# Retention in 64-column tiles of the array: padded queries, key halves, one retention step per filler

## The chip, the cores and the metric

The kernel runs on one core of one Trainium2 chip. The metric is device time in microseconds of one launch, median of several runs. A core has five engines with a queue of instructions each: TensorE (PE, matrix products; PEld is its loading of weights), VectorE (DVE), ScalarE (ACT), GpSimd (POOL) and SyncE (SP), which here issues nearly all DMA transfers. TensorE writes to PSUM, which is eight banks of 128 partitions; VectorE and ScalarE take results out of it.

## The reference

Eight batches of 576 tokens. First retention with 8 heads of 64: causal, decaying scores without a softmax. Its output goes through an attention with 4 experts of which 2 are chosen per token, and then through a token and channel mixer (last lines left out here).

```python
gamma = 1.0 - 2.0 ** (-5.0 - np.arange(H))
rel = pos[:, None] - pos[None, :]
Dmat = np.where(rel >= 0, gamma[:, None, None] ** rel[None, :, :], 0.0)
ret = scale * np.matmul(q, k.transpose(0, 1, 3, 2)) * Dmat[None]
x = np.matmul(ret, v)                 # 8 batches x 8 heads x 576 x 64
# then, per expert e: q, k, v = x @ wq[e], x @ wk[e], x @ wv[e]
#   a = softmax(causal(q @ k.T / 8)); out += gate_e * (a @ v @ wo[e])
# then theta = x @ w_theta; y = w_tok_r @ (x cos theta) + w_tok_i @ (x sin theta)
#   u = x + y; result = u + relu(u @ w_ch)
```

The inputs of the three parts are independent of the kernel's tiling; only retention is touched by the change.

## The kernel before

The program has two halves. The first does retention, projections and attention for batch after batch; the second (from about 560 us) is the mixer. In the first half the attention of batch b runs as 10 units (2 pairs of experts x 5 row chunks), and beside it, as fillers, the second pair's projections of batch b and then retention, values and first projections of batch b+1. `fill` takes fillers off a list by cost numbers until the share of the batch is done. What is issued is then set in its final order, engine by engine, by the framework's scheduler, so instructions of neighbouring pieces are interleaved.

Retention works in 5 chunks of 128 rows (the last has 64), `ROWS`. Heads go in pairs: head pair hp (0 to 3) has two heads s, whose 64 dimensions lie in partitions 0 to 63 and 64 to 127.

- `loads(b, c)` (L95): one DMA brings queries and keys `qk`, transposed, one DMA brings rows of keys and values `kv`; GpSimd scales values into `vp` (L102). Three buffers each; the loads of a chunk are issued at the end of the output of the chunk three before.
- `ret_scores` (L106): for each head a product of 64 contraction rows, keys (128 columns) by queries (128), L113. A matmul on half the array's rows leaves the other half to the other head. The two heads of a pair go to two PSUM tiles `w`. VectorE multiplies each tile with the triangle `tri` into `sm` (L117). The quarter of keys above 64 by queries under 64 is computed and then zeroed.
- `ret_out` (L121): keys by values are added to the running state in PSUM `pS` (L130, 64-column tiles, one head in columns 0 to 63 of the array and one in 64 to 127); ScalarE copies the state into a block-diagonal `S` (L135, two copies, the rest of `S` is zero from the start). The output tile `w` collects state times queries (L139, the whole array, 128 columns of weights) and `vp` times `sm` (L143, 64-column tiles). VectorE multiplies with the decay into `xt` (L150), ScalarE and GpSimd split it (L152, L153).

PSUM holds four tiles `a` for attention, three `w` (`WB`) for retention and projections, and `pS`. Around these, TensorE runs the attention: scores L258 (`KK`, whole array) and L261 (`KL`, half the rows), transposes of the probabilities `P` L310, attention output L329 (64-column tiles), and projections L83 to L85. VectorE takes the scores' maxima (L264), scales `P` (L283), and copies transposed tiles (L315, L317).

All products of retention are float32, which TensorE runs as two passes; a trace shows each pass as a matmul with a weight load.

Of the kernel before, what the change touches and what calls it, by code (L numbers as in the profile page):

```python
# [20 lines left out]
E, DM = 4, 512  # L21
# [6 lines left out]
NCONST = 256 + NCH * H + 1088 + E * E + 4 * (128 + NCH)  # L28
# [25 lines left out]
def tile_kernel(ctx: ExitStack, tc: tile.TileContext, qk, kv, w1, wo, wot, wd, cst, out):  # L54
# [17 lines left out]
    tri = att.tile([128, 128], F32, name="tri")  # L72
# [7 lines left out]
    SB = [ret.tile([128, 4, 128], F32, name=f"S{i}") for i in range(2)]  # L80
# [14 lines left out]
    def loads(b, c):  # L95
        R = ROWS[c]
        t = ret.tile([128, 2, 4, R], F32, name="qk", bufs=LDB, padded_shape=[128, 2, 4, 128])
        nc.sync.dma_start(t, qk[b, :, c * 1024:c * 1024 + 8 * R].rearrange("p (a h r) -> p a h r", a=2, h=4))
        u = ret.tile([128, 2, DM], F32, name="kv", bufs=LDB)
        nc.sync.dma_start(u[:R], kv[b, c * C:c * C + R, :].rearrange("r (a d) -> r a d", a=2))  # L100
        vp = ret.tile([128, H, D], F32, name="vp", bufs=VPB)
        MARK["pool"] = nc.gpsimd.tensor_mul(vp[:R], u[:R, 1, :].rearrange("p (h d) -> p h d", h=H),  # L102
                             gam[:R, c, :, None].to_broadcast([R, H, D]))
        QKT[b, c], KVT[b, c], VP[b, c] = t, u, vp

    def ret_scores(b, c):  # L106
        R = ROWS[c]
        t, u = QKT[b, c], KVT[b, c]
        ps = [ps1.tile([128, 4, R], F32, name="w", bufs=WB, padded_shape=[128, 4, 128]) for _ in range(2)]
# [4 lines left out]
        sm = []  # L114
        for s in range(2):
            m = ret.tile([128, 4, R], F32, name="sm", bufs=3, padded_shape=[128, 4, 128])
            nc.vector.tensor_mul(m[:R], ps[s][:R], tri[:R, None, :R].to_broadcast([R, 4, R]))  # L117
            sm.append(m)
        SM[b, c] = sm

    def ret_out(b, c):  # L121
        R = ROWS[c]
        t, u, vp, sm = QKT.pop((b, c)), KVT.pop((b, c)), VP.pop((b, c)), SM.pop((b, c))
# [34 lines left out]
    def ret_fill(b):  # L158
        L = []
        for c in range(NCH + 1):  # L160
            if c < NCH:
                L.append((1.74, lambda c=c: ret_scores(b, c)))
# [602 lines left out]
```

## Time and profile before

| | us |
|---|---|
| runs | 998.91, 1000.17, 998.31; median 998.91 |
| span of the profiled execution | 994.0 |
| PE busy | 964.6 (97%) |
| PEld busy | 857.6 (86%) |
| DVE busy | 677.7 (68%) |
| ACT busy | 499.9 (50%) |
| POOL busy | 221.9 (22%) |

The profiled execution lists its span, from the first to the last instruction; the runs' times hold what lies around it as well. A busy share is an average over stages. In the chain of waits, which is followed back from the last instruction, each piece is what the span was waiting for at that moment; a piece named "issue" is time in which the engine waited for nothing that the profile shows.

### The profile page before, as it was taken

Reading aid. Unit: us, or ns where it says so; the run is one execution under the profiler, and the core shown is the slowest. Engines: PE = TensorE matmul, PEld = TensorE weight load, DVE = VectorE, ACT = ScalarE, POOL = GpSimd, SP = SyncE. Lnnn points to the kernel's source line nnn. Section 1 sums busy time; section 2 is a strip of 40 time slices with the busy share of each in tenths; the row PEclk is TensorE's granted clock in tenths of the full one; section 3 lists DMA queues with packets and bytes.
Section 4 is the critical chain, followed back from the end, with each engine's and each line's share of the span. In section 5 each row is a group of like instructions: output and inputs, shape, how many; then the busy total and the mean of one; then the engine's idle time right before and its main releaser. Section 6 shows DMA issues by size and latency. Waiting matters only on the chain.

```text
span 994.0 us, 20992 instructions
## 1 busy us (share of the span) xinstructions
PE 964.6 (97%) x7898; PEld 857.6 (86%) x7898; DVE 677.7 (68%) x2035; ACT 499.9 (50%) x1310; POOL 221.9 (22%) x270
## 2 busy tenths in 40 slices
PE   7999999999999999999999999999999999999998
PEld 6978878788787887887867799999999999999998
DVE  6387897878777878778566793485655746486533
ACT  3366676666664766667566661344333432344320
POOL 4244262352532623423000002020100102020110
PEclk9999999999998999999999999999999999999999
DMA  9454573554544635443641301010000101000001
GB/s 308 153 155 150 144 211 82 161 174 134 173 124 118 217 100 155 161 133 112 251 150 36 122 1 48 2 72 25 25 24 24 49 1 48 2 36 13 25 25 48
DMA packets 58293, 99.27 MB, mean 100 GB/s; under 512 B 13904, under 2 KB 35792, under 8 KB 58192
## 3 DMA queue, kind: packets, MB, share of 16 engines
q1 hardware_dynamic: 58048, 97.65, 31.2%
q8 instruction: 62, 1.02, 0.4%
q0 software_dynamic: 144, 0.28, 0.1%
q14 instruction: 39, 0.32, 0.1%
HBM read 65.09 MB, written 23.66 MB: 89 GB/s over the span
## 4 chain that ended last, share of the span: by engine, by line
PE 88%; DVE 5%; DMA 2%; ACT 2%; issue 2%; SPq 0%; ACTq 0%; DVEq 0%
PE acc L641 23%; PE w L83 12%; PE w L84 11%; PE w L85 11%; PE a L329 5%; PE a L310 5%; PE w L113 4%; PE a L258 3%; PE w L143 3%; PE a L261 3%; PE w L139 2%; PE acc L631 2%; PE pS L130 1%; DMA qk<-qk 1%; DVE P L283 1%
## 5 line engine op out<-in xcount | busy, mean ns | idle before, releaser
L641 PE MATMUL acc<-TK,zh 128*128 128x256 f32 (+1 forms) x1024 | 183.8, 302 | 0.0
L641 PEld LDWEIGHTS acc<-TK,zh 128*128 128x128 f32 x1024 | 152.4, 190 | 0.7 <-DVE ul L89 0.2
L667 POOL TENSOR_TENSOR o<-o,ul 128x576 f32<-128x576 f32 x28 | 41.8, 1499 | 436.1 <-DVE o L662 436.1
L269 ACT ACTIVATE P<-P,st 128x128 f32<-128x128 f32 (+4 forms) x160 | 95.6, 599 | 72.2 <-DVE st L264 71.8
L641 PE MATMUL acc<-TK,zl 128*128 128x256 f32 (+1 forms) x512 | 110.0, 297 | 0.0
L264 DVE CUSTOM_DVE_ANT_0 P<-a,cm 128x128 f32<-128x128 f32 (+4 forms) x160 | 72.3, 478 | 49.7 <-PE a L261 49.1
L641 PEld LDWEIGHTS acc<-TK,zl 128*128 128x128 f32 x512 | 86.2, 189 | 0.1
L585 ACT ACTIVATE cs<-cs 128x512 f32<-128x512 f32 x72 | 45.2, 630 | 80.4 <-DVE cs L583 76.7
L88 ACT ACTIVATE zh<-cs 128x512 fp32r<-128x512 f32 x64 | 40.2, 630 | 81.3 <-PE acc L641 66.9
L89 DVE TENSOR_TENSOR zl<-cs,zh 128x512 fp32r<-128x512 f32 x64 | 45.0, 707 | 50.4 <-ACT zh L88 49.5
L83 PE MATMUL w<-xh,WH 128*128 128x288 f32 x256 | 79.0, 308 | 0.0
L84 PE MATMUL w<-xl,WH 128*128 128x288 f32 x256 | 76.4, 299 | 0.0
L84 PE MATMUL w<-ul,CH 128*128 128x256 f32 (+1 forms) x256 | 75.9, 296 | 0.0
L83 PE MATMUL w<-uh,CH 128*128 128x256 f32 (+1 forms) x256 | 75.9, 296 | 0.0
L85 PE MATMUL w<-uh,CH 128*128 128x256 f32 (+1 forms) x256 | 75.9, 296 | 0.0
L85 PE MATMUL w<-xh,WL 128*128 128x288 f32 x256 | 75.7, 296 | 0.0
L587 DVE SCALAR_TENSOR_TENSOR cs<-cs,x 128x512 f32<-128x512 f32 x72 | 55.4, 776 | 24.6 <-ACT cs L585 24.5
L310 PE MATMUL a<-ident,P 128*128 128x128 f32 (+2 forms) x480 | 63.4, 264 | 7.8 <-DVE P L283 6.2
L113 PE MATMUL w<-qk 64*128 64x128 f32 (+1 forms) x640 | 59.1, 277 | 10.8 <-issue 5.6
L113 PEld LDWEIGHTS w<-qk 64*128 64x128 f32 (+1 forms) x640 | 50.8, 180 | 18.2 <-issue 10.5
L89 DVE TENSOR_TENSOR ul<-acc,uh 128x256 fp32r<-128x256 f32 x64 | 25.7, 451 | 59.3 <-ACT uh L88 59.1
L117 DVE TENSOR_TENSOR sm<-w,tri 128x512 f32<-128x512 f32 (+1 forms) x80 | 49.6, 629 | 21.6 <-PE w L113 11.4
(139 smaller groups left out, 2466.6 us busy)
## 6 DMA issues: line engine op xcount, KB each, us to landing
qk<-qk SPq DMA_DIRECT2D x32, 512.0 KB, 4.6
kv<-kv SPq DMA_DIRECT2D x32, 512.0 KB, 3.9
KK<-KN SPq DMA_DIRECT2D x64, 144.0 KB, 2.5
raw<-wd SPq DMA_DIRECT2D x43, 192.0 KB, 2.7
out<-o SPq DMA_DIRECT2D x28, 288.0 KB, 2.1
td<-hl SPq DMA_DIRECT2D x27, 192.0 KB, 2.3
TK<-td SPq DMA_DIRECT2D x9, 576.0 KB, 6.9
od<-ob SPq DMA_DIRECT2D x16, 288.0 KB, 2.6
```

The source lines that it names most:

```text
L83: nc.tensor.matmul(ps, ah, bh, start=first, stop=False)
L84: nc.tensor.matmul(ps, ah, bl, start=False, stop=False)
L85: nc.tensor.matmul(ps, al, bh, start=False, stop=last)
L89: nc.vector.tensor_sub(l, src, h)
L113: nc.tensor.matmul(ps[s][:R, hp, :], t[sl, 1, hp, :], t[sl, 0, hp, :], start=True, stop=True)
L117: nc.vector.tensor_mul(m[:R], ps[s][:R], tri[:R, None, :R].to_broadcast([R, 4, R]))
L264: MARK["dve"] = nc.vector.tensor_tensor_reduce(Ps[s][:R, j0:j1], ps[s][:R], cm[:R, o + j0:o + j1], 1.0, st[:R, 0, s:s + 1] if i else 3.0e3 ...
L269: MARK["act"] = nc.scalar.activation(Ps[s][:R, :n], Ps[s][:R, :n], AF.Exp, bias=st[:R, last, s:s + 1], scale=-1.0, accum_out=st[:R, 2, s:s ...
L310: nc.tensor.transpose(tp[:w, j, :], Ps[s][:R, j * C:j * C + w], ident[:R, :R])
L329: nc.tensor.matmul(po[s * 64:s * 64 + 64, c0:], V[:ROWS[j], j, 2 * p + s, :], v, start=j == 0, stop=j == last, skip_group_check=True)
L587: nc.vector.scalar_tensor_tensor(z, cs, -1.0, x2[:, None, ds].to_broadcast([128, 2, 256]), op0=OP.mult, op1=OP.mult)
L641: nc.tensor.matmul(acc[d][j], A[:, dc], TK[:, kt, W, t0:t1], start=q == 0 and n == 0, stop=q == 8 and n == 2)
```

## The change

Every product of retention now has 128 contraction rows and 64 columns of weights.

- Queries go to `QZ`, three fixed buffers with two planes: plane s holds the queries of head s in its 64 partitions and zeros in the other 64. The zeros are written once, at the start, by GpSimd. One load of `qk` becomes three: two of queries (64 partitions each) and one of keys, `kt`.
- Scores: weights are 64 keys of both heads of a pair (128 rows), the queries of both planes stream side by side: 2 x 128 columns for the first 64 keys, 2 x 64 for the second 64, which skip the queries under 64. The halves alternate between the left and right 64 columns of the array. Odd head pairs have their key halves swapped in the PSUM partitions, and so `kv` and the decay table are swapped for them on the host. The rows of the last chunk's `kv` are padded to 128.
- Masks: four VectorE instructions instead of two per chunk (two for the last chunk), into fixed tiles `SMT` whose unseen quarter is zeroed once.
- State: `S` is 64 columns wide and no longer block-diagonal: ScalarE copies it in one instruction. State times queries is one product per head with that head's plane, 64 columns of weights.
- `ret_fill` gives one filler per chunk, scores of chunk c and output of chunk c-1, where these were two; the cost numbers are lower.

```diff
     def loads(b, c):
...
+        qz = QZ[(b * NCH + c) % LDB]
+        for s in range(2):
+            sl = slice(s * 64, s * 64 + 64)
+            nc.sync.dma_start(qz[sl, s, :, :R], qk[b, sl, o:o + 4 * R].rearrange("p (h r) -> p h r", h=4))
...
     def ret_scores(b, c):
...
-        for hp in range(4):
-            for s in range(2):
-                sl = slice(s * 64, s * 64 + 64)
-                nc.tensor.matmul(ps[s][:R, hp, :], t[sl, 1, hp, :], t[sl, 0, hp, :], start=True, stop=True)
-        for s in range(2):
-            nc.vector.tensor_mul(m[:R], ps[s][:R], tri[:R, None, :R].to_broadcast([R, 4, R]))
+        for i in range(2):
+            for e, j in ((0, 0), (1, 0), (1, 1), (0, 1)):
+                if j * 64 < R:
+                    g = slice((e ^ j) * 64, (e ^ j) * 64 + 64)
+                    hp = 2 * i + e
+                    nc.tensor.matmul(ps[e][g, i, :, j * 64:R], t[:, hp, j * 64:j * 64 + 64],
+                                     qz[:, :, hp, j * 64:R], start=True, stop=True, skip_group_check=True)
+        for e in range(2):
+            g = slice(e * 64, e * 64 + 64)
+            nc.vector.tensor_mul(sm[e][g, :, :, :64], ps[e][g, :, :, :64],
+                                 tri[g, 2, None, None, :].to_broadcast([64, 2, 2, 64]))
+            if R > 64:
+                nc.vector.tensor_mul(sm[e][:, :, :, 64:], ps[e][:, :, :, 64:],
+                                     tri[:, e, None, None, :].to_broadcast([128, 2, 2, 64]))
...
     def ret_out(b, c):
...
-            Sn = SB[(c + 1) % 2]
-            for s in range(2):
-                sl = slice(s * 64, s * 64 + 64)
-                nc.scalar.activation(Sn[sl, :, sl], pS[sl], AF.Copy)
+            nc.scalar.activation(SB[(c + 1) % 2], pS, AF.Copy)
...
-            nc.tensor.matmul(px[:, hp, :], Sb[:, hp, :], t[:, 0, hp, :], start=hp == 0, stop=False,
-                             skip_group_check=True)
+            for s in range(2):
+                nc.tensor.matmul(px[s * 64:s * 64 + 64, hp, :], Sb[:, hp, :], qz[:, s, hp, :R],
+                                 start=hp == 0, stop=False, skip_group_check=True)
...
     def ret_fill(b):
...
-                L.append((1.74, lambda c=c: ret_scores(b, c)))
...
-                L.append((2.9, lambda c=c: ret_out(b, c - 1)))
+        return [((1.4 if c < NCH else 0) + (2.5 if c else 0), lambda c=c: step(c)) for c in range(NCH + 1)]
```

In the order of instructions a name is the tile written, an arrow, the tiles read; the shape is that of the result, and a number behind x counts equal neighbours. The lines of the new kernel are other ones: its scores are L125, keys by values L146, state L153, outputs L157, attention L272, L275, L324, L343, masks L130 and L133, and L164 the decay.

TensorE, third batch's retention, from the first scores to the third. Before:

```order
L85 MATMUL w<-xh,WL 128x288
L113 MATMUL w<-qk 128x128 x16
L329 MATMUL a<-PT,V 64x128 x2
L258 MATMUL a<-KK,U 128x384 x2
L261 MATMUL a<-KL,U 128x384 x2
L310 MATMUL a<-ident,P 128x128 x4
L130 MATMUL pS<-vp,kv 64x64 x8
L143 MATMUL w<-sm,vp 64x128 x8
L113 MATMUL w<-qk 128x128 x4
```

After, from the end of the first scores:

```order
L125 MATMUL w<-qz_109,kt 64x256 x2
L125 MATMUL w<-qz_109,kt 64x2x64 x2
L343 MATMUL a<-PT,V 64x128 x2
L272 MATMUL a<-KK,U 128x384 x2
L275 MATMUL a<-KL,U 128x384 x2
L324 MATMUL a<-ident,P 128x128 x4
L125 MATMUL w<-qz_110,kt 64x256 x2
L125 MATMUL w<-qz_110,kt 64x2x64 x2
L125 MATMUL w<-qz_110,kt 64x256 x2
L125 MATMUL w<-qz_110,kt 64x2x64 x2
L146 MATMUL pS<-vp,kv 64x64 x8
```

The scores of chunks 0 and 1, sixteen neighbours before, now have the attention's pieces between them.

TensorE, the same batch, scores of chunk 3 and output of chunk 2. Before:

```order
L113 MATMUL w<-qk 128x128 x2
L310 MATMUL a<-ident,P 128x128 x8
L113 MATMUL w<-qk 128x128 x6
L130 MATMUL pS<-vp,kv 64x64 x8
L139 MATMUL w<-qk,S_107 128x128 x4
L143 MATMUL w<-sm,vp 64x128 x8
L258 MATMUL a<-KK,U 128x128 x2
```

After:

```order
L125 MATMUL w<-qz_109,kt 64x256
L324 MATMUL a<-ident,P 128x128 x8
L125 MATMUL w<-qz_109,kt 64x256
L125 MATMUL w<-qz_109,kt 64x2x64 x2
L125 MATMUL w<-qz_109,kt 64x256 x2
L125 MATMUL w<-qz_109,kt 64x2x64 x2
L146 MATMUL pS<-vp,kv 64x64 x8
L153 MATMUL w<-qz_111,S_107 64x128 x8
L157 MATMUL w<-sm_114,vp 64x128 x2
```

From the scores to the outputs all rows now are 64 high; before, the height and the operands' rows change at each line. The transposes still cut into the scores.

VectorE at the start of the same batch's retention. Before:

```order
L283 TENSOR_SCALAR P<-P,st 128x256
L194 SCALAR_TENSOR_TENSOR U<-w,U 64x288 x2
L117 TENSOR_TENSOR sm<-w,tri 128x512 x3
L264 ISA P,st<-a,cm 128x384
L264 ISA st 128x1
L264 ISA P,st<-a,cm 128x384
L264 ISA st 128x1
L315 COPY PT<-a 128x2x128
```

After:

```order
L297 TENSOR_SCALAR P<-P,st 128x256
L208 SCALAR_TENSOR_TENSOR U<-w,U 64x288 x2
L130 TENSOR_TENSOR sm_114<-w,tri 64x4x64
L133 TENSOR_TENSOR sm_114<-w,tri 128x4x64
L130 TENSOR_TENSOR sm_115<-w,tri 64x4x64
L133 TENSOR_TENSOR sm_115<-w,tri 128x4x64
L278 ISA P,st<-a,cm 128x384
L278 ISA st 128x1
L278 ISA P,st<-a,cm 128x384
L278 ISA st 128x1
L329 COPY PT<-a 128x2x128
L130 TENSOR_TENSOR sm_112<-w,tri 64x4x64
```

Three masks of 512 columns stood ahead of the attention's maxima; now the four of one chunk do, and the next chunk's four come behind.

## Rows read from the trace of the kernel before

**Rows 1.** The page's busy time of TensorE and its weight loads, others behind.

```profile
PE 964.6 (97%) x7898; PEld 857.6 (86%) x7898; DVE 677.7 (68%) x2035; ACT 499.9 (50%) x1310; POOL 221.9 (22%) x270
```

**Rows 2.** Busy time by stage: the start, three of seven retention stretches, sum of seven.

```profile
core 0: us, PE busy (x) PEld busy (x) DVE busy (x) ACT busy (x) POOL busy (x), PEclk, DMA share, GB/s
0.00:30.00 30.00, 23.90 (x313) 21.69 (x314) 17.61 (x25) 10.41 (x18) 13.38 (x19) 1.00 0.91 304
...
175.00:207.20 32.20, 30.83 (x349) 25.39 (x349) 26.69 (x93) 21.41 (x60) 15.62 (x20) 1.00 0.61 190
238.00:270.00 32.00, 28.50 (x304) 23.40 (x306) 25.96 (x81) 18.54 (x53) 12.44 (x15) 0.95 0.55 162
306.00:338.00 32.00, 30.64 (x314) 24.70 (x314) 26.57 (x86) 19.35 (x55) 14.72 (x18) 0.89 0.53 165
...
sum 225.20, PE 213.24 PEld 173.61 DVE 189.19 ACT 143.76 POOL 97.80; mean PE 30.46 PEld 24.80 DVE 27.03 ACT 20.54 POOL 13.97
```

**Rows 3.** Chain of waits, 176 to 206 us: start, us, what, passes.

```profile
176.64 1.14 PE w L113 x16
177.78 1.18 issue
178.96 1.83 PE w L113 x16
...
182.66 0.61 PE pS L130 x16
183.28 0.88 PE w L143 x16
...
188.34 0.62 DVE P L283
...
189.87 0.45 PE w L139 x4
...
196.86 1.09 PE w L139 x8
197.95 1.02 PE w L143 x16
...
200.22 0.61 PE w L113 x16
```

**Rows 4.** Waits, 49 to 500 us: who for whom, us in total, times, longest.

```profile
PEld w L113 <- issue: 10.5, 22, 1.4
PE a L310 <- DVE P L283: 6.2, 9, 2.1
PE w L113 <- issue: 5.6, 5, 1.2
```

**Rows 5.** Chain of waits, single pieces of three other stretches.

```profile
16.40 6.72 DMA qk<-qk
...
128.53 1.08 PE a L329 x12
...
257.35 2.51 DVE P L283
```

**Rows 6.** Groups by shape: count, busy us, mean ns of one, idle before.

```profile
L117 DVE TENSOR_TENSOR sm<-w,tri 128x512 f32<-128x512 f32 x64 | 43.1, 685 | 18.3 <-PE w L113 11.4 <-PE w L143 6.2 <-PE a L261 0.4
L117 DVE TENSOR_TENSOR sm<-w,tri 64x256 f32<-64x256 f32 x16 | 6.5, 407 | 3.3 <-PE w L143 3.3
L264 DVE CUSTOM_DVE_ANT_0 P<-a,cm 128x256 f32<-128x256 f32 x32 | 12.5, 422 | 13.9 <-PE a L261 13.9
L135 ACT ACTIVATE S<-pS 64x256 f32<-64x256 f32 x64 | 24.1, 377 | 2.8 <-PE pS L130 2.3
L347 POOL MEMSET S<- 128x512 f32 x2 | 1.0, 524 | 0.3 <-POOLq L757 0.3
```

**Rows 7.** Issues of line L98: ns least, median, most; first and last start.

```profile
L98 SPq DMA_DIRECT2D qk<-qk x40: 327/358/562, 1.2 to 450.5; - x40
```

**Rows 8.** Weight loads of line L143, the same columns.

```profile
L143 PEld LDWEIGHTS w<-sm,vp x640: 128/137/231, 10.0 to 467.7; 128*64 128x64 f32 x128, 64*64 64x64 f32 x32
```

More of the change, by code (lines that the diff above doesn't have):

```diff
@@ L71, in tile_kernel @@
     ident = consts.tile([128, 128], F32, name="ident")
-    tri = att.tile([128, 128], F32, name="tri")
+    tri = att.tile([128, 3, 64], F32, name="tri")
     gam = att.tile([128, NCH, H], F32, name="gam")
@@ L79, in tile_kernel @@
     gt = ret.tile([128, 4, S], F32, name="gt")
-    SB = [ret.tile([128, 4, 128], F32, name=f"S{i}") for i in range(2)]
+    SB = [ret.tile([128, 4, D], F32, name=f"S{i}") for i in range(2)]
+    QZ = [ret.tile([128, 2, 4, 128], F32, name=f"qz{i}") for i in range(LDB)]
+    SMT = [[ret.tile([128, 2, 2, 128], F32, name=f"sm{i}{e}") for e in range(2)] for i in range(2)]
     def mm3(ps, ah, al, bh, bl, first, last):
@@ L96, in loads @@
         R = ROWS[c]
-        t = ret.tile([128, 2, 4, R], F32, name="qk", bufs=LDB, padded_shape=[128, 2, 4, 128])
-        nc.sync.dma_start(t, qk[b, :, c * 1024:c * 1024 + 8 * R].rearrange("p (a h r) -> p a h r", a=2, h=4))
+        qz = QZ[(b * NCH + c) % LDB]
+        o = c * 1024
+        for s in range(2):
+            sl = slice(s * 64, s * 64 + 64)
+            nc.sync.dma_start(qz[sl, s, :, :R], qk[b, sl, o:o + 4 * R].rearrange("p (h r) -> p h r", h=4))
+        t = ret.tile([128, 4, R], F32, name="kt", bufs=LDB, padded_shape=[128, 4, 128])
@@ L104, in loads @@
-        QKT[b, c], KVT[b, c], VP[b, c] = t, u, vp
+        MARK["pool"] = nc.gpsimd.tensor_mul(vp, u[:, 1, :].rearrange("p (h d) -> p h d", h=H),
+                                            gam[:, c, :, None].to_broadcast([128, H, D]))
+        QKT[b, c], KVT[b, c], VP[b, c] = (qz, t), u, vp
     def ret_scores(b, c):
         R = ROWS[c]
-        t, u = QKT[b, c], KVT[b, c]
-        ps = [ps1.tile([128, 4, R], F32, name="w", bufs=WB, padded_shape=[128, 4, 128]) for _ in range(2)]
-        for hp in range(4):
-            for s in range(2):
-                sl = slice(s * 64, s * 64 + 64)
-                nc.tensor.matmul(ps[s][:R, hp, :], t[sl, 1, hp, :], t[sl, 0, hp, :], start=True, stop=True)
@@ L114, in ret_scores @@
-        sm = []
-        for s in range(2):
-            m = ret.tile([128, 4, R], F32, name="sm", bufs=3, padded_shape=[128, 4, 128])
-            nc.vector.tensor_mul(m[:R], ps[s][:R], tri[:R, None, :R].to_broadcast([R, 4, R]))
-            sm.append(m)
+        qz, t = QKT[b, c]
+        ps = [ps1.tile([128, 2, 2, 128], F32, name="w", bufs=WB) for _ in range(2)]
+        for i in range(2):
[5 more added lines that the diff above has]
+                                     qz[:, :, hp, j * 64:R], start=True, stop=True, skip_group_check=True)
@@ L158, in ret_fill, with step @@
     def ret_fill(b):
-        L = []
-        for c in range(NCH + 1):
+        def step(c):
             if c < NCH:
-                L.append((1.74, lambda c=c: ret_scores(b, c)))
+                ret_scores(b, c)
             if c:
-                L.append((2.9, lambda c=c: ret_out(b, c - 1)))
-        return L
+                ret_out(b, c - 1)
+        return [((1.4 if c < NCH else 0) + (2.5 if c else 0), lambda c=c: step(c)) for c in range(NCH + 1)]
     QKP, VB, GW = {}, {}, {}
@@ L343, in tile_kernel @@
         nc.tensor.matmul(pw, warm, warm, start=True, stop=True)
-    o = 256
+    o = 448
     nc.sync.dma_start(gam, cst[:, o:o + NCH * H].rearrange("p (c h) -> p c h", c=NCH))
-    for s in SB:
-        nc.gpsimd.memset(s, 0.0)
+    for s in range(2):
+        for q in QZ:
+            nc.gpsimd.memset(q[64 - 64 * s:128 - 64 * s, s], 0.0)
+        for sm in SMT:
+            nc.gpsimd.memset(sm[s][64 - 64 * s:128 - 64 * s, :, :, :64], 0.0)
     for l in LG:
@@ L712, in prep @@
     qk = np.ascontiguousarray(np.concatenate(blocks, axis=2))
-    kv = np.ascontiguousarray(np.concatenate([rows(k), rows(v)], axis=2))
+    kv = np.zeros((B, NCH * C, 2 * DM), f)
+    kv[:, :S] = np.concatenate([rows(k), rows(v)], axis=2)
+    kv = kv.reshape(B, NCH, 2, 64, 2, 2, 2, 128)
+    kv[:, :, :, :, :, :, 1] = kv[:, :, ::-1, :, :, :, 1].copy()
+    kv = np.ascontiguousarray(kv.reshape(B, NCH * C, 2 * DM))
     parts = []
@@ L732, in prep @@
     cst[:, 0:128] = np.eye(128)
-    cst[:, 128:256] = np.triu(np.ones((128, 128)))
-    pos = np.arange(NCH)[None, :, None] * C + np.arange(128)[:, None, None]
+    tri = np.triu(np.ones((64, 64)))
+    cst[0:64, 256:320], cst[64:128, 256:320] = 1.0, tri
+    cst[0:64, 320:384], cst[64:128, 320:384] = tri, 1.0
+    cst[0:64, 384:448], cst[64:128, 384:448] = tri, tri
+    swap = 64 * (np.arange(H) // 2 % 2)
+    pos = np.arange(NCH)[None, :, None] * C + (np.arange(128)[:, None, None] ^ swap)
     gamma = 1.0 - 2.0 ** (-5.0 - np.arange(H))
-    o = 256
+    o = 448
     cst[:, o:o + NCH * H] = (gamma ** -pos.astype(np.float64)).reshape(128, -1)
```

18 lines of the change are left out of this document (9 added, 9 removed).

## The prediction

> **What bounds the kernel now.** I read first the totals: TensorE is busy 964.6 of 994.0 us, no other engine over 68% [rows 1]. Then the busy time by stage: retention runs in seven stretches of some 32 us beside the attention of the batch before (an eighth, batch 0, stands alone in the first 30 us). In these stretches TensorE is busy 213.2 of 225.2 us and VectorE 189.2, 84% [rows 2]; outside them retention does nothing, so the change can only act there. Then the chain of waits in one stretch [rows 3]: almost every piece is TensorE's, so a TensorE nanosecond saved is a span nanosecond until VectorE becomes late. Two pieces are not: an idle 1.18 us between the two first score blocks, and 0.62 us of `P` scaling that the transposes wait for. The first recurs in the batches (10.5 us of weight-load idle and 5.6 us of matmul idle before L113 in 49 to 500 us, with the smaller waits in it; [rows 4]). I put the large gap between those two blocks at 7 us over seven batches, by the row's 1.18 rounded down for the batch in which attention stands between the blocks.
>
> Each fp32 matmul is two passes, so `x16` in the chain is 8 matmuls.
>
> **Prices from rows.** All in the stretch of rows 3 unless named.
> - 64-column tile, 64 columns streamed: `pS`, 16 passes 0.61 with the change of shape before it; less 0.14 (below) 0.47.
> - 64-column tile, 128 columns: L143 straight behind `pS`, 16 passes 0.88, 0.055 a pass.
> - 64-column tile, 256 columns: L329, 12 passes 1.08 [rows 5]; four of them have 128 columns (0.22), so eight cost 0.86, 0.108 a pass.
> - Full array, state times queries: L139 straight behind transposes, 4 passes 0.45, 0.11 a pass, 0.90 for eight.
> - Change of shape: L143 behind L139 takes 1.02 where behind `pS` it takes 0.88: 0.14 for entering 64-column tiles. L139 behind `pS` takes 1.09 against 0.90: 0.19 for entering the full array. I take 0.14 for tiles, half-row work and transposes, 0.19 for all 128-column weights.
> - Scores before: blocks whose two PSUM tiles alternate take 1.14 with their entry, 0.056 a pass; a block that the order has sorted by PSUM tile (eight passes into one, then the other) takes 1.83, 0.112 a pass.
>
> **Part by part.**
> *Scores.* In the order 166 of 256 full-size score matmuls alternate and 90 do not: 166 x 0.112 + 90 x 0.224 = 38.7 us, and the eight 64-key blocks at 0.47 each [0.61 in rows 3] with some lone matmuls 4.2: 43. After: 8 passes of 256 columns and 8 of 128 are 0.86 + 0.44 = 1.30 a chunk, 41.6 for 32; last chunks 8 x 0.44 = 3.5; where the order cuts a block into odd pieces a pass has no partner, 20 times, 3 us: 48. So the scores alone become **5 us dearer**. Leaving out the unseen quarter does not pay for padding the queries.
> *State.* 32 products: 0.90 each, 28.7 us. After: 24 of 0.88, eight last ones (64 columns) of 0.47, six odd cuts: 25.6, **-3.1**. Key-value products are cut oddly 14 times, +0.6, the rest -0.4. Streaming in all +2.3 us.
> *Changes of shape.* I counted in the whole order of TensorE where shape differs from the instruction before: 466 before, 415 after. By kind: `pS` 32 to 10, outputs 33 to 0, attention outputs 53 to 45 (0.14 each); state 25 at 0.19 to 11 at 0.14; scores 39 at 0.19 to 49 at 0.14; query-key 78 to 64 and projections 48 to 59 (0.19); transposes 53 to 70, key-low 105 to 107 (0.14). Sum **-10.5 us**.
> *The wait between score blocks.* Scores 0 and 1 stood back to back and the second waited for a PSUM tile `w`; now attention output, a query-key pair and four transposes lie between, about 0.2 + 0.5 + 0.4 + 0.6 = 1.7 us of TensorE by the pieces of rows 3, while VectorE frees the tile. **-7 us** if nothing else becomes late.
> *VectorE.* Two masks of 0.685 a chunk become two of 64x256 (0.407) and two of 128x256 (0.422, by the row of that shape) [rows 6]: +0.29 x 32 = 9 us, 1.2 a stretch, on an engine that idles 5 us in each stretch [rows 2]. On the path only where TensorE waits for it; I charge 5 us of the 17.5 won for that, since the stretch would shrink by about 2 us while VectorE grows by 1: 28.2 busy in 30.2, 93%.
> *Off the path.* ScalarE copies the state once instead of twice (0.377 saved a chunk [rows 6]), nobody waits. GpSimd's scaling of the last chunk has 128 rows for 64, eight times in all; GpSimd is busy 22% [rows 1], nothing. Memsets: two of 0.524 become ten smaller ones, at most 5 us behind 0.7, by the size of that one [rows 6], while the scores wait for loads anyway; nothing.
> *Loads.* Two more issues on SP's queue a chunk, 0.358 each [rows 7], 29 us in all on a queue that stands in order ahead of `KK`, `raw` and `td`. The loads of a chunk are issued behind the output three chunks before, so I take nothing; if one chunk a batch came late by its two issues, 0.7 x 7 = 5 us. In the first 30 us the DMA engines are 0.91 busy and the scores wait for queries until 23.1 [rows 2, 5]; 256 KB more of last-chunk rows at 304 GB/s are 0.8 us. Batch 0's shape changes after that give about as much back: 0, between -1 and +2.
>
> **Sum.** +2.3 - 10.5 - 7 + 5 = -10.2. One thing more: the granted clock is 0.95 and 0.89 in two stretches [rows 2], behind a 2.51 us wait for the scaling of `P` [rows 5]; shares of 1.2 GHz among 2.4; these cost 32 x (0.05 + 0.11) = 5 us. With an idle of 1.2 us less in each stretch I count half of that as gone, -2.5. In all **-12.7**: span 994.0 to 981.3, median 998.9 to 986.2. (The runs' times are 4.9 us over the profiled span; I carry that unchanged.)
>
> **A rule against the change.** TensorE's passes in 64-column tiles with 128 rows come at 0.055 us a pass while one weight load takes 0.137 [rows 3, 8], so loads run beside matmuls. The Trainium skill, TensorE: Matmul & The Clock Gate, Part 3, says that weight loads overlap running matmuls only where the row groups differ; here all row groups are the same. By that rule every pass in such a tile would cost its load (rival 4). The rows of `pS` and of L143 speak against it: 16 passes in 0.47 and 0.88, where 16 loads of 0.137 would be 2.2.
>
> **Rivals.**
> 1. *The wait moves.* VectorE frees the score tiles in time but then scales `P` later, and the transposes wait instead (0.62 already in rows 3). All 7 us go back, and the clock stays: 998.9 - 8.2 + 1 = 991.7. For it: four mask instructions now stand in one row on VectorE ahead of the maxima of the next scores.
> 2. *VectorE becomes the bound (slower).* Its idle 5 us a stretch are latency that cannot be squeezed, so the added 9 us lie on the path whole: 1008. It decides where VectorE reaches about 95% of a stretch; against it, TensorE waits for VectorE in these stretches only some microseconds in all now [rows 4]. The Trainium skill, TensorEngine Tiling (Array Packing), Performance Considerations, says that tiling speeds TensorE up but not the emptying of PSUM, which may become the bottleneck: this rival.
> 3. *Everything is won and both clock dips go:* 998.9 + 2.3 - 10.5 - 7 - 5 = 978.7, with VectorE's 5 us not paid.
> 4. *It doesn't do what it says:* the weight loads of the new tiles wait for the running matmul. 576 passes of scores and 512 of state at a load of 0.137 [rows 8] are 149 us against the 74 priced above: 986 + 75 = 1061. The queries of two heads' halves in one operand, two runs of 128 or 64, are a shape that no row shows; if such passes streamed at half speed the 48 us of scores would double: 1034.
>
> **How the numbers follow.** Forecast 986 (982 to 991): 0.55. Rival 1, 992 (991 to 998): 0.2. Rival 3, 979 (976 to 982): 0.12. Rival 2, 1008: 0.1. Rival 4: 0.02 for the loads, 0.01 for the runs. A difference under 0.2%, 2 us, is what a measurement of this kernel can't tell from none. Within it lies the end of rival 1, 0.05, with the near end of rival 2, 0.01; slower is 0.12; faster the rest, 0.82. The range leaves out rivals 2 and 4 and the ends of 1 and 3: 978 to 998.
>
> **What would show it.** TensorE's busy time down by 8 to 9 us and its pieces in the chain: scores 1.3 to 1.45 a block, state 0.88 with no 0.2 ahead of it, `pS` 0.47, output 0.88; no idle between the first two score blocks; VectorE some 9 us busier, 90% or more in the stretches; waits of transposes for the scaling of `P` up by a few microseconds. I would be wrong if pairs of 256-column passes take over 0.25, if score blocks wait for `qz` or `kt` landings, or if the transposes' waits grow by over 10 us.

## The result: 988.6 us for 998.8

The changed kernel takes 988.6 us in the median (984.1 to 995.7) against 998.8 (992.2 to 1006.0) for the kernel before; the ratio is 0.9895, 95% interval 0.9872 to 0.9918. The forecast of 986.2 was close. The experiments show that it was close with the credit in the wrong place, and so in part by luck: the order of the fillers won some 18 us, and the tiles, with their loads and masks, gave about 8 back.

The page's busy time after, as in [rows 1], and the chain's shares by engine:

```profile
PE 958.8 (97%) x8090; PEld 848.1 (86%) x8090; DVE 683.4 (69%) x2099; ACT 487.1 (49%) x1278; POOL 226.7 (23%) x278
...
PE 83%; DVE 10%; DMA 3%; issue 1%; ACT 1%; SPq 1%; POOL 1%; ACTq 0%; POOLq 0%
```

TensorE is 5.8 us less busy (forecast 8 to 9), VectorE 5.7 more (forecast 9). VectorE's share of the chain was 5% in the kernel before; it is 11% in e1 below, which is faster than either, so this share alone says little. Busy time of three of after's seven stretches, from first scores to last output, and the sum of the seven:

```profile
core 0: us, PE busy (x) PEld busy (x) DVE busy (x) ACT busy (x) POOL busy (x), PEclk, DMA share, GB/s
...
178.20:209.30 31.10, 29.13 (x372) 23.00 (x371) 30.15 (x94) 18.83 (x54) 16.86 (x20) 0.96 0.72 216
241.70:270.50 28.80, 28.40 (x372) 22.05 (x371) 26.25 (x93) 18.29 (x52) 15.82 (x20) 1.00 0.71 213
...
367.50:400.30 32.80, 29.96 (x372) 22.94 (x371) 29.91 (x94) 18.40 (x53) 15.98 (x20) 0.97 0.63 197
...
sum 213.80, PE 203.53 PEld 158.89 DVE 195.78 ACT 127.59 POOL 106.77; mean PE 29.08 PEld 22.70 DVE 27.97 ACT 18.23 POOL 15.25
```

Against [rows 2] (where the windows were cut a little wider) VectorE has gone from 84% to 92% of the stretch. In the first of these three it is busy 30.15 of 31.10 us, and the chain of waits there, nearly all TensorE in [rows 3], is now VectorE's, piece behind piece, until TensorE gets its scaled `P`:

```profile
198.34 0.60 DVE xt L164
198.94 0.42 DVE P L297
199.37 0.17 DVE ex L413
...
200.52 0.34 DVE sm L130
200.88 0.43 DVE sm L130
...
203.72 0.98 DVE P L297
204.71 0.28 DVE b L412
205.01 0.26 DVE ex L413
205.30 0.70 DVE xt L164
206.03 0.63 ACT xh L166
206.66 0.21 ACT ob L347
206.92 0.48 PE a L324
207.40 1.05 PE w L153 x16
208.45 0.85 PE w L157 x16
```

That is this one stretch in this one execution. In the second profile of after, taken below, the same stretch takes 29.40 us and its chain is mostly TensorE's; another stretch (from 366 us) is mostly VectorE's in both.

TensorE's own prices came out as forecast: a score block with its entry 1.45 and `pS` 0.47 (in the chain of e8, shown below, whose products are after's), state 0.88, output 0.89, from the chain of after's batch 0:

```profile
23.36 1.52 PE w L125 x16
24.88 0.88 PE w L153 x16
25.75 0.89 PE w L157 x16
```

Where the time went, line by line on TensorE: each matmul's time is taken as its end less the end of the one that ended before it, so that waits count, and added up by kind from the first attention score to the first mixer product. Batch 0's retention lies ahead of that, so retention's rows hold the other seven batches. In the kernels with the new score tiles neighbouring kinds overlap: taken in the order of starts instead, after's scores come to 50.5, its `pS` to 12.8 and its state to 27.8, while the sum of the four rows of retention falls by 1 only.

| us | before | after | after, second profile | e1 (one filler) | e5 (e1, three loads) | e3 (after, old scores) | e9 (e1, four masks) | e15 (after, all quarters) |
|---|---|---|---|---|---|---|---|---|
| up to the first attention score | 43.6 | 46.0 | 47.1 | 44.4 | 48.5 | 48.4 | 42.9 | 45.1 |
| scores | 56.2 | 48.3 | 48.2 | 38.0 | 36.8 | 39.6 | 38.4 | 59.5 |
| `pS` | 18.3 | 17.1 | 16.8 | 17.7 | 17.2 | 18.5 | 18.5 | 15.1 |
| state | 29.1 | 25.8 | 23.2 | 30.1 | 28.7 | 24.1 | 33.7 | 23.6 |
| output | 33.1 | 30.4 | 28.7 | 32.8 | 31.9 | 28.8 | 34.4 | 28.5 |
| transposes | 63.7 | 68.8 | 68.5 | 63.4 | 63.4 | 69.0 | 71.2 | 61.8 |
| attention, projections | 315.8 | 317.4 | 319.4 | 316.5 | 318.7 | 317.8 | 321.8 | 320.0 |
| mixer | 434.2 | 434.0 | 433.9 | 434.0 | 433.9 | 434.4 | 434.2 | 433.8 |
| span | 994.0 | 987.7 | 986.0 | 976.8 | 979.3 | 980.6 | 995.1 | 987.5 |

### The profile page after: what moved, and what is told of

Same layout as the page of the kernel before. It is cut to its first block, busy times and chain, and to the rows that moved or that the text cites. A ratio compares the mean times of both kernels' runs of the same rounds, so it can differ in the third digit from the quotient of the medians.

```text
span 987.7 us, 21586 instructions
## 1 busy us (share of the span) xinstructions
PE 958.8 (97%) x8090; PEld 848.1 (86%) x8090; DVE 683.4 (69%) x2099; ACT 487.1 (49%) x1278; POOL 226.7 (23%) x278
## 3 DMA queue, kind: packets, MB, share of 16 engines
q1 hardware_dynamic: 63936, 99.79, 33.1%
## 4 chain that ended last, share of the span: by engine, by line
PE 83%; DVE 10%; DMA 3%; issue 1%; ACT 1%; SPq 1%; POOL 1%; ACTq 0%; POOLq 0%
PE acc L658 24%; PE w L87 12%; PE w L88 11%; PE w L89 11%; PE a L343 4%; PE a L324 4%; PE a L272 3%; PE a L275 2%; PE w L125 2%; PE w L157 2%; PE w L153 2%; PE acc L648 2%; DMA kv<-kv 2%; DVE P L278 2%; DVE sm L130 1%
## 5 line engine op out<-in xcount | busy, mean ns | idle before, releaser
L324 PE MATMUL a<-ident,P 128*128 128x128 f32 (+2 forms) x480 | 65.2, 265 | 11.1 <-DVE P L297 5.2
L125 PE MATMUL w<-qz,kt 128*64 128x256 f32 (+1 forms) x576 | 61.8, 334 | 7.7 <-DMA kt<-qk 5.1
L167 POOL TENSOR_TENSOR xl<-xt,xh 128x512 fp32r<-128x512 f32 (+1 forms) x40 | 50.7, 1269 | 78.8 <-ACT xh L166 78.8
L324 PEld LDWEIGHTS a<-ident,P 128*128 128x128 f32 (+2 forms) x480 | 45.7, 138 | 26.1 <-DVE P L297 7.4
```

The lines of the kernel that those rows point to most:

```text
L125: nc.tensor.matmul(ps[e][g, i, :, j * 64:R], t[:, hp, j * 64:j * 64 + 64], qz[:, :, hp, j * 64:R], start=True, stop=True, skip_group_check ...
L167: nc.gpsimd.tensor_sub(xl[:, :, cs], xt, xh[:, :, cs])
L324: nc.tensor.transpose(tp[:w, j, :], Ps[s][:R, j * C:j * C + w], ident[:R, :R])
```

## Experiments

Theory at the start: the gain is removed waits and changes of shape, less VectorE's lateness and a slower start. Rivals: it is the order of the fillers alone, or the tiles alone, or less time at the lower clock. Each ratio below is to runs of the kernel before in the same series; since these drift (their medians go from 994 to 997), ratios compare better across series than medians do.

| | median us | ratio to before, 95% | mean clock, median of its runs |
|---|---|---|---|
| after, second series | 985.6 | 0.9895 (0.9872 to 0.9918) | 0.996 |
| e1 before, one filler per chunk | 978.4 | 0.9817 (0.9791 to 0.9843) | 0.996 |
| e11 the same, old cost numbers | 976.3 | 0.9808 (0.9756 to 0.9859) | 0.997 |
| e2 after, two fillers per chunk | 1005.3 | 1.0091 (1.0066 to 1.0115) | 0.992 |
| e3 after, scores of before | 983.5 | 0.9871 (0.9844 to 0.9897) | 0.987 |
| e5 e1 with three loads | 980.8 | 0.9816 (0.9781 to 0.9851) | 0.991 |
| e9 e1 with four masks | 993.6 | 0.9955 (0.9924 to 0.9986) | 0.990 |
| e15 after with all quarters, two masks | 987.1 | 0.9915 (0.9882 to 0.9948) | 0.993 |
| e8 after, scaling on ScalarE | 990.3 | 0.9927 (0.9896 to 0.9958) | 0.992 |
| e10 e1, scaling on ScalarE | 976.5 | 0.9776 (0.9740 to 0.9812) | 0.995 |
| e14 e3, scaling on ScalarE | 986.3 | 0.9905 (0.9871 to 0.9940) | 0.983 |
| e16 e9, scaling on ScalarE | 1003.6 | 1.0083 (1.0051 to 1.0115) | 0.984 |

**The order or the tiles.** e1 merges the fillers of the kernel before and leaves all else:

```diff
...
-                L.append((1.74, lambda c=c: ret_scores(b, c)))
...
-                L.append((2.9, lambda c=c: ret_out(b, c - 1)))
...
+        return [((1.4 if c < NCH else 0) + (2.5 if c else 0), lambda c=c: step(c)) for c in range(NCH + 1)]
```

> The kernel before with one thing of the change: a chunk's scores and the output of the chunk before it form one filler, with the cost numbers of after. Tiles, masks, loads and state are those of before. Its order alternates the two PSUM tiles in 125 of 128 score pairs of 128 columns (before 83) and puts attention's pieces between the first two score blocks. By the prices of the prediction, TensorE's retention and attention products stream 153.4 us (before 163.3, after 165.6) and shape changes cost 80.6 (81.1, 71.0). Theory A (the gain is mostly the order's): 10 us below before by these prices and up to 7 more by the wait between the first two score blocks, 982 to 989 at a before of 998.8: as fast as after or faster. Rival B (the gain comes from the new tiles and their fewer shape changes): within 3 us of before, 996 to 1000. Rival C (the gain is that less time is spent at the lower clock): the time follows the granted clock, not the prices.

e11 is e1 with 1.74 and 2.9:

> e1 (before with one filler per chunk) with the cost numbers of before (1.74 and 2.9, added) in place of 1.4 and 2.5. Its TensorE order has the same 125 alternating score pairs and the same attention pieces between the first two score blocks as e1. Theory A (merging the fillers is what pays, by the order of the score blocks): as e1, 976 to 981. Rival K (the lower cost numbers pay, since retention is taken off the list later or earlier): 990 to 999, near before.

e2 is after with the old list of fillers (the diff above backwards):

> The kernel after with the old list of fillers, scores and output apart with the old cost numbers: the new tiles, masks, loads and state without the new order. Streaming by the prices 165.5 us, shape changes 74.1: 239.6 against 244.4 before and 236.6 after. Theory A (order pays): 4.8 us below before by prices, less 2.5 for the three loads at the start and 0 to 5 for VectorE's four masks: 996 to 1001, about 8 to 12 us slower than after. Rival B (the tiles pay): 988 to 992, within 3 us of after.

And after once more:

> The kernel after once more, unchanged, beside the three others on the same chip and with a second profile. Expected 988.6 within 3 us in the median, single runs from 984 to 996 as before, with the time falling as the mean granted clock rises (995.7 at 0.988, 984 at 0.997): 1 per cent of clock for 1.2 per cent of time. If the second profile again has two transposes' waits for VectorE of 1 to 2 us in most batches, these belong to the kernel and not to the one execution.

Theory A held in all three, though two numbers missed its ranges. By their ratios e1 and e11 are 18 to 19 us faster than before and 8 to 9 faster than after: merging alone is worth more than the whole change, and the cost numbers make no difference that the runs show. e1, at 978.4, is below the 982 to 989 that I gave it. With the old order (e2) the new tiles are a loss of 8.5 us against before, where I had put e2 between 996 and 1001, about level with it. The second series of after, 985.6, is at the edge of what I expected. TensorE's groups by line, 49 to 500 us, show what the order does (busy, mean ns of one, idle before; the scores L113 and the transposes L310 of before, then of e1, then L324 and L125 of after; last, the transposes of e2 and of e11):

```profile
L310 PE MATMUL a<-ident,P 128*128 128x128 f32 (+2 forms) x421 | 55.2, 265 | 7.6 <-DVE P L283 6.2 <-DVE st L264 0.6 <-ACT ob L333 0.3
L113 PE MATMUL w<-qk 64*128 64x128 f32 (+1 forms) x560 | 52.2, 278 | 7.1 <-issue 5.6 <-PE w L113 0.8 <-DVE U L194 0.6
```

```profile
L310 PE MATMUL a<-ident,P 128*128 128x128 f32 (+2 forms) x440 | 57.2, 263 | 7.9 <-DVE P L283 5.7 <-DVE st L264 2.0
...
L113 PE MATMUL w<-qk 64*128 64x128 f32 (+1 forms) x560 | 38.9, 275 | 1.6 <-DVE sm L117 1.6
```

```profile
L324 PE MATMUL a<-ident,P 128*128 128x128 f32 (+2 forms) x424 | 57.5, 266 | 10.8 <-DVE P L297 5.2 <-ACT ob L347 2.8 <-DVE st L278 2.7
L125 PE MATMUL w<-qz,kt 128*64 128x256 f32 (+1 forms) x504 | 53.6, 329 | 0.0
```

```profile
L324 PE MATMUL a<-ident,P 128*128 128x128 f32 (+2 forms) x410 | 55.4, 266 | 19.5 <-DVE P L297 10.1 <-ACT ob L347 6.0 <-DVE st L278 2.7
L310 PE MATMUL a<-ident,P 128*128 128x128 f32 (+2 forms) x440 | 57.6, 264 | 10.2 <-DVE P L283 7.6 <-DVE st L264 2.0 <-ACT ob L333 0.6
```

The same 560 score passes cost 13.3 us less in e1, with 5.5 less idle before them. The order explains both: the first two score blocks stand apart, so no block waits right behind another, and the heads alternate in 125 of 128 pairs where the kernel before has 83 and runs the rest tile by tile, at twice the price [rows 3]. In the trace of before it is the second score block of a batch (batch 0's aside) that alternates only in part, and the third that doesn't alternate at all, in all eight batches. Why the scheduler orders a block one way or the other (I take it to be which PSUM tiles are free) no run shows. After's scores then cost 14.7 more than e1's.

The idle time before the transposes is 7.6, 7.9 and 10.8, and 19.5 in e2, where the two fillers come back. Part of it is ScalarE's: of after's 3.2 more than before, 2.5 come from ScalarE's copies of the attention output (`ob`), and the wait for the scaling of `P` is less (5.2 for 6.2). This idle doesn't rank the kernels by itself either: e11, one of the two fastest, has 10.2.

The second profile of after shows the same waits (3.9, 3.7 and 2.1 us before transposes, by the same three releasers), so they are the kernel's. That time falls with the clock held only roughly: 984.6 and 987.9 both stand at 0.995.

**Scores, state and loads, one at a time.** e3 is after with the scores and masks of before:

```diff
...
-                    nc.tensor.matmul(ps[e][g, i, :, j * 64:R], t[:, hp, j * 64:j * 64 + 64],
-                                     qz[:, :, hp, j * 64:R], start=True, stop=True, skip_group_check=True)
...
+                nc.tensor.matmul(ps[s][:R, hp, :], t[sl, hp, :], qz[sl, s, hp, :R], start=True, stop=True)
...
```

> The kernel after with the scores of before: half the array's rows for each head, 128 keys of weights, all four quarters computed, two masks per chunk. Kept of the change: padded queries, three loads, the state in 64-column tiles, one filler per chunk. Streaming by the prices 148.9 us, shape changes 72.4: 221.3 against 236.6 after. Theory A (order pays, and the score part of the change is a loss): 15 us below after, and VectorE's 6 to 9 us of extra masks gone with some 3 us of transposes' waits: 970 to 976. Rival B (scores in 64-column tiles are what pays): slower than after, 990 to 996. Rival C (VectorE's wait between the first score blocks decides): 985 to 990, since both have the same places.

e5 is e1 with its one load of queries and keys in three pieces:

```diff
-        nc.sync.dma_start(t, qk[b, :, c * 1024:c * 1024 + 8 * R].rearrange("p (a h r) -> p a h r", a=2, h=4))
+        o = c * 1024
+        for s in range(2):
+            sl = slice(s * 64, s * 64 + 64)
+            nc.sync.dma_start(t[sl, 0], qk[b, sl, o:o + 4 * R].rearrange("p (h r) -> p h r", h=4))
+        nc.sync.dma_start(t[:, 1], qk[b, :, o + 4 * R:o + 8 * R].rearrange("p (h r) -> p h r", h=4))
```

> e1 (before with one filler per chunk) and one thing more of the change: a chunk's queries and keys come in three transfers, as in after, and into the same tile as in e1 (no zero planes). Everything else as e1, 978.4. Theory A (three loads cost time at the start, where scores wait for them): batch 0's stretch ends at 34.0 us in e3 and at 29.9 in e1, and the granted clock of 20 to 40 us is 0.83 there against 1.00; so 3 to 5 us more than e1, 981 to 983.5, nearly all of it before 40 us. Rival B (e3 is slower than e1 by the zero planes, their memsets or by VectorE alone): within 1 us of e1, 977.4 to 979.4.

e3 missed: 983.5 for 970 to 976. TensorE did what the prices said, but the time didn't follow. In the table, scores, `pS`, state and output of e3 take 111.0 us against 114.6 in e5 and 118.6 in e1, yet its transposes take 5.6 more, and the start 4.0 more than e1's. So the state in 64-column tiles with its padded queries, e3 against e5, saves 3.6 us on retention's lines and loses 5.6 at the transposes, whose idle time is 12.7 us in e3 and 7.1 in e5. A stretch of e3 shows VectorE without any room:

```profile
177.90:207.20 29.30, 26.58 (x380) 21.30 (x379) 28.83 (x85) 18.55 (x54) 15.66 (x20) 1.00 0.71 219
```

By the ratios, of the 8 us that after loses to e1 some 5 come with what e3 keeps (padded queries, loads, state) and some 2 with the score tiles and masks, though e3's and after's intervals overlap.

e5 is 2.4 us over e1 in the median, just under what A said, but its ratio is the same (0.9816 and 0.9817): the runs don't show that three loads cost time in the end. What shows is the place: batch 0's retention ends at 34.1 us, in e1 at 29.9, and the first attention score comes 4.1 us later; 1.6 of that comes back behind. The fourth chunk's one load of queries and keys lands at 19.8 us in e1; in e5 the last of its three lands at 23.2, in e3 at 23.5. What the start costs is seen in busy times by stretch, of e3 and then of e1:

```profile
20.00:23.60 3.60, 0.19 (x8) 0.05 (x2) 3.60 (x5) 2.48 (x4) 0.49 (x2) 0.74 1.06 274
23.60:27.00 3.40, 3.33 (x28) 3.14 (x30) 0.74 (x2) 0.00 (x0) 2.22 (x2) 0.50 1.08 307
```

```profile
20.00:24.00 4.00, 3.27 (x40) 2.79 (x40) 4.00 (x5) 0.63 (x1) 2.71 (x2) 1.00 0.73 155
24.00:27.00 3.00, 2.97 (x40) 2.70 (x40) 1.50 (x3) 1.33 (x3) 2.36 (x3) 1.00 0.90 345
```

In e3 TensorE stands idle for 3.4 of 3.6 us, until the fourth chunk's keys have landed and VectorE, busy throughout, is done with a piece that ends 0.13 us later; then TensorE's granted clock is 0.50, that is 1.2 GHz, while it works through what has waited.

**The masks and the quarter.** e9 is e1 with after's four masks:

```diff
...
-            nc.vector.tensor_mul(m[:R], ps[s][:R], tri[:R, None, :R].to_broadcast([R, 4, R]))
...
+            nc.vector.tensor_mul(m[:64, :, :64], ps[s][:64, :, :64], tri[:64, None, :64].to_broadcast([64, 4, 64]))
+            if R > 64:
+                nc.vector.tensor_mul(m[:, :, 64:], ps[s][:, :, 64:], tri[:, None, 64:].to_broadcast([128, 4, 64]))
...
```

> e1 with the masks of after: for each head's score tile one instruction of 64x256 and one of 128x256 into fixed tiles whose unseen quarter is zeroed once, in place of one of 128x512. TensorE's products are those of e1. VectorE is busy 9 to 10 us more over the span (32 x 2 x (0.41 + 0.41 - 0.68)). Theory V (with the new order VectorE sets the pace of the stretches: it is busy 26 of 28.5 us in them): most of it lies on the path, 5 to 9 us more than e1, 983.5 to 987.5. Rival T (TensorE sets the pace, VectorE's work is hidden): 0 to 2 us more, 978 to 980.5.

It costs 14 (by the ratios) to 15 us, far beyond the 5 to 9 of theory V. VectorE has only 5.2 us more work in the profile (674.3 for 669.1), and it is busy for 85% of e9's seven stretches (189 of 222 us), in e1 for 89% (183 of 207): it doesn't run out of time, its pieces come late. How is read from the transposes' row, 49 to 500 us, from the chain behind one of these waits, and from the busy times there:

```profile
L313 PE MATMUL a<-ident,P 128*128 128x128 f32 (+2 forms) x420 | 54.1, 263 | 15.1 <-DVE P L286 14.6 <-DVE st L267 0.5
```

```profile
183.73 1.23 DVE P L286
184.96 0.04 issue
185.00 0.88 PE a L313 x6
185.88 0.61 PE pS L133 x16
186.49 1.77 PE w L142 x8
188.26 1.91 PE w L146 x16
```

```profile
184.00:186.00 2.00, 1.00 (x12) 0.83 (x14) 2.00 (x3) 0.85 (x3) 1.81 (x2) 1.00 0.06 23
186.50:190.50 4.00, 4.00 (x30) 3.62 (x32) 3.10 (x13) 2.73 (x7) 1.34 (x3) 0.57 0.33 66
```

The transposes wait 14.6 us for the scaling of `P`, 11 times, where e1 has 5.7. And after such a wait the state products take 1.77 and the outputs 1.91, where [rows 3] has 1.09 and 1.02: the granted clock of those 4 us is 0.57. So a wait can be paid twice. By the traces' records of the granted clock from 12 to 560 us, TensorE runs at 1.2 GHz for 31 us in all in this execution of e9, in eight stretches, all close behind an idle of 0.86 to 2.0 us; for 7 us in e1, 10 in before, 17 in after (10 in its second profile), 20 in e3. At half speed each microsecond of that loses up to half: 15 us in e9, 3 in e1. This execution of e9 was one of its slower ones (996.8, mean clock 0.985). By the medians of the mean clock, 0.990 and 0.996, the clock is worth some 5 us between e9 and e1; that is an estimate, and with the 9 us more of waits for the scaling it comes near e9's loss. e9's order on TensorE changed a little with the masks as well, so the masks are not shown to be the only cause.

e15 is after with the unseen quarter computed and two masks of 128x512:

```diff
...
-                    nc.tensor.matmul(ps[e][g, i, :, j * 64:R], t[:, hp, j * 64:j * 64 + 64],
-                                     qz[:, :, hp, j * 64:R], start=True, stop=True, skip_group_check=True)
+                    nc.tensor.matmul(ps[e][g, i, :, :R], t[:, hp, j * 64:j * 64 + 64],
+                                     qz[:, :, hp, :R], start=True, stop=True, skip_group_check=True)
...
```

> after with the unseen quarter computed: the second 64 keys too meet all 128 queries of both heads (2x128 columns where there were 2x64), and each score tile has one mask of 128x512, as before, in place of one of 64x256 and one of 128x256. By the prices TensorE's retention and attention products with their shape changes cost 245.3 us against 236.6 (scores 62.3 for 48.3, other pieces 5 less); VectorE has some 9 us less. Theory V (the two extra masks cost more than the quarter saves): within 3 us of after or faster, 978 to 988. Theory T (TensorE's products set the time): 992 to 996.

Theory V held: 0.9915 against 0.9895, no difference that the intervals show. TensorE's groups, 49 to 500 us:

```profile
L125 PE MATMUL w<-qz,kt 128*64 128x256 f32 (+1 forms) x504 | 64.7, 378 | 0.0
L321 PE MATMUL a<-ident,P 128*128 128x128 f32 (+2 forms) x426 | 56.6, 266 | 5.6 <-DVE P L294 3.3 <-ACT ob L344 1.6 <-DVE st L275 0.6
```

Scores are 11 us dearer (64.7 for 53.6), and the transposes' idle falls from 10.8 to 5.6; in the table their whole time falls by 7.0. `pS`, state and output fall by 6.1 together (against the second profile by 1.5), attention and projections rise by 2.6. In all, leaving out the quarter wins TensorE about what the two extra masks take from it.

**Taking work off VectorE.** Four kernels have `NDVE = ()` for `(0,)`: ScalarE scales `P` for both experts.

> after with the scaling of the probabilities of both experts on ScalarE, where VectorE scaled those of one: 40.8 us of work leaves VectorE (683), some 48 come to ScalarE (487). In a stretch VectorE falls from 28.0 to about 25 us and ScalarE rises from 18.2 to about 21. Theory V (VectorE sets the pace of after's stretches; TensorE's transposes wait for it): stretches shrink toward TensorE's own 28 us and the transposes' waits for VectorE, 5 to 8 us, go: 978 to 984 against 985.6. Rival T (TensorE sets the pace, or the waits are latency that ScalarE has too): 985 to 990.

> e1 with the scaling of the probabilities of both experts on ScalarE. In a stretch VectorE falls from 26.2 to about 23 us, ScalarE rises from 20.3 to about 23.5. Theory V: TensorE's idle time in e1's stretches (28.5 us long, 27.6 busy at full clock) is VectorE's lateness, so up to 0.9 us a stretch is to be had, and the stretches at lower clock recover: 970 to 976 against 978.4. Rival T: no gain or a loss, as ScalarE now does in a row what two engines did side by side: 978 to 984.

> e3 (after with the scores of before, two masks) with the scaling of the probabilities of both experts on ScalarE. e3 has TensorE's cheapest order (221.3 us by the prices against 234.0 of e1) but its transposes wait 8.0 us for VectorE's scaling, and its time is 983.5. Theory V (VectorE's lateness takes the gain of the state tiles): those waits go and some of the 12.7 us come out, 972 to 979. Rival T (the start and the low clock take them, or ScalarE is as late): 981 to 986.

> e9 (e1 with four masks, 993.6) with the scaling of the probabilities of both experts on ScalarE. In e9 the transposes wait 14.6 us for VectorE's scaling against 5.7 in e1. Theory V (the masks stand ahead of the scaling in VectorE's row and delay it): the waits go with the scaling, 976 to 983. Rival O (e9's time is its changed TensorE order, with some lone score passes and more shape changes, 236.8 us by the prices against 234.0; this kernel's order costs 241.9): 986 or more.

Theory V in its simple form, that VectorE alone sets the pace, fell in three of four; e10 lies between the ranges of V and T. e8 takes 42 us off VectorE (641.4 for 683.4) and isn't faster. A stretch of e8 at full clock:

```profile
240.40:269.20 28.80, 28.65 (x372) 21.99 (x371) 24.05 (x87) 20.51 (x57) 16.12 (x20) 1.00 0.71 211
```

and the start of the chain of its stretch before:

```profile
178.11 1.45 PE w L125 x16
179.56 0.22 PE a L343 x4
179.78 0.55 PE a L272 x2
180.33 0.38 PE a L275 x2
180.71 0.58 PE a L324 x4
181.29 1.45 PE w L125 x16
182.74 0.47 PE pS L146 x16
183.21 0.88 PE w L157 x16
```

VectorE is down to 24.05, and the stretch has the same 28.80 us as after's beside the same time: there TensorE, busy 28.40 and now 28.65 of it, was nearer to its limit than VectorE with 26.25. In e14 and e16 the scaling on ScalarE is late in its turn: the transposes wait 9.0 and 14.4 us for `P` of ScalarE, 8.0 and 14.6 for VectorE's in e3 and e9. e16's 10 us over e9 go rival O's way, though by the prices its order is dearer by 5 us only (241.9 for 236.8). What delays the scaling is then not VectorE's load alone; which part of it is the order in which the scheduler puts the scaling, and which the engines' work ahead of it, these runs don't settle. e10, at 976.5, shows no gain clear of e1 and e11 (ratio 0.9776 against 0.9817 and 0.9808; the intervals overlap). e1, e5, e10 and e11 beat both kernels.

## Why the prediction held, and which steps did not

The prediction's terms, put together by kind of product as in the table (streaming, its changes of shape and its waits; VectorE's charge at the transposes):

| after less before, us | forecast | measured | second profile |
|---|---|---|---|
| scores (+5.0 streaming, -0.5 shape, -7 wait) | -2.5 | -7.9 | -8.0 |
| state (-3.1, -3.2 shape) | -6.3 | -3.3 | -5.9 |
| `pS` (+0.6, -3.1 shape) | -2.5 | -1.2 | -1.5 |
| output (-0.4, -4.6 shape) | -5.0 | -2.7 | -4.4 |
| transposes (+2.4 shape, +5 VectorE) | +7.4 | +5.1 | +4.8 |
| attention and projections, shape | -1.4 | +1.6 | +3.6 |
| start | 0 | +2.4 | +3.5 |

The columns add up to -10.3 (the prediction's -10.2), -6.0 and -7.9; the spans of the profiles differ by 6.3 and 8.0 us, the medians of the runs by 10.2. The forecast's terms are for eight batches, the measured rows of retention for seven. Those four rows together fell by 15.1 and 19.8 us for a forecast of 16.3, so retention's own lines won about what was forecast, the split between them being less sure. The misses lie beside them, at the start and in attention and projections, and the transposes' charge was on the high side. Errors of both signs cancel in the sum: that it came near the runs is in part luck.

- **Scores.** New blocks cost what was forecast, 1.45. The term of the sum was mis-sized on the other side: the old blocks, 56.2 us in seven batches, were dearer than my 43 with their changes of shape and waits. And the +5 mixed two things. The tile-by-tile blocks of before, about 10 us (90 x 0.112), were not the old tiles' fault but the order's, and the merged filler alone takes them away (e1: -18 on scores). Against alternating old blocks the new ones are 10 us dearer (48.3 for 38.0). Had I priced the old scores in the new order, I would have seen that the tiles lose: by the same prices e1 costs 234.0 us and after 236.6, before VectorE's charge.
- **The wait between score blocks, -7.** Right in size and cause: idle before the scores 7.1 before, 1.6 in e1, 0.0 after.
- **Changes of shape, -10.5.** The step whose gain didn't arrive. The matmuls behind them did get cheaper in part (state, `pS` and output -7.2, in the second profile -11.8, forecast with their streaming -13.8). But e3, with 8 us less of changes of shape than e1 by the prices and scores nearly as cheap, is no faster than e5, which has about as many as before: 5.6 us went to waits before the transposes. A saving on TensorE counted in the span here only until another engine was late, and the charge of 5 stood against the wrong sum. That VectorE is the late engine fits e3's stretch above; e14, where ScalarE scales instead, waits for ScalarE and is no faster, so what makes the scaling late stays open.
- **VectorE, +9 busy, +5 on the path.** Busy +5.7; idle before the transposes +3.2, of which 1.1 are VectorE's. The sign that I had named, more waits for the scaling of `P`, did not come: 5.2 us for 6.2, in the second profile 3.9. So rival 1's wait did not move there. Rival 2 appears in single stretches of the chain, but in e1's chain too. What was not priced is the clock behind a wait. The Trainium skill's warning (TensorEngine Tiling (Array Packing), Performance Considerations: the emptying of PSUM may become the bottleneck) fits e15, where two mask instructions a chunk cost about what the columns saved. That emptying PSUM was the bottleneck here is not shown: e8, with 42 us less on VectorE, is no faster.
- **Clock, -2.5.** The runs bear out its sign, the first profile does not. Before's runs have a median mean clock of 0.991 to 0.993 in three series, after's 0.993 and 0.996. The profiled execution of before, at 0.995, was one of its better ones, with 10 us at the lower clock; after's first profile has 17, its second 10. The second profile, with as much lowered time as before's, is 8.0 us shorter, the medians lie 10.2 apart; that the rest is the clock is an estimate. I had put both dips of before behind the wait for `P` [rows 5]. The records of the granted clock put one of them, at 260.9 us, behind that wait and the other, at 312.1, behind 1.24 us of idle TensorE between the first two score blocks, which the change removes.
- **Start, 0 between -1 and +2.** Measured +2.4 and +3.5, above the range. I had priced the extra bytes (0.8 us) and not the order of the issues: the fourth chunk's queries and keys land at 19.0 us in before and at 23.2 in after, behind its three loads, as in e5. A sign of being wrong that I had named came with it: score blocks wait 5.1 us for landings of `kt` (6.6 in the second profile), all in the first batch, where before's waited 3.7 for `qk`.
- **What lies around the span, 4.9 us.** Mis-sized: the runs listed with their spans lie 1.7 to 2.2 us over them. The profiled execution of before was then a run of about 996, at the low end of its 992 to 1006, and some 3 of the 4.9 us that I carried were that.
- **Rival 4** fell: 16 state passes take 0.88 and 16 of output 0.89 in after's chain, a score block 1.45; 16 loads of 0.137 [rows 8] would be 2.2. The rule of the Trainium skill behind it (TensorE: Matmul & The Clock Gate, Part 3: loads overlap matmuls only where row groups differ) doesn't agree with this trace, where all row groups are the same. The same part also lets a load into a background weight buffer run ahead; no row here tells which buffer a load goes to.

## What to carry to other kernels

Price a new tile shape against the old one in the same order: if a change also moves instructions, time the move alone first; here it was the whole gain. Where two engines were each over 90% of the stretches, as in e3 and after, cheaper instructions on one came back as waits for another, and adding work to the second to save columns on the first was a draw (e15 against after). A wait of TensorE of a microsecond or two could cost more than itself here, where the granted clock fell behind it. A single profile can be an untypical execution: compare its mean clock with that of the runs first.

## What the hardware showed unexpectedly

- All 23 stretches at 1.2 GHz in six profiles (before, after, e1, e3, e9, e11; 12 to 560 us) came close behind an idle TensorE of 0.86 to 3.5 us, or during one. The reverse doesn't hold: of 57 idles of 0.9 us or more there, 22 were followed by such a stretch. The same 1.34 us of idle, between 495 and 517 us, was followed by one in e3, e9 and e11 and by none in before, after and e1. In e9 the same state products took 1.77 us in such a stretch for 1.09.
- Splitting each mask of 128x512 (0.68 us) into 64x256 and 128x256 (0.42 and 0.41 us in after) raised VectorE's busy time by 5 us and, with the order that the scheduler made of it, the kernel's time by 14 to 15 (e9 against e1).
- Query operands that are two runs of 128 columns in two planes stream as fast as one run: 16 score passes with their entry take 1.45 us, the forecast's 1.30 and 0.14.
